# Gated mix of two 32-head attentions on one core: the load order of the first phase, and a scale chain of its own for the values' weights and the gate

## The chip, the cores and the metric

The kernel runs on 1 core of one Trainium2 chip. The metric is the device time of one launch in microseconds (us). The time before is 2800.9 us, the median of 3 runs (2800.7 to 2802.06). A difference of less than 0.2% (5.6 us) counts as no change here.

## The reference, cut to what matters

Two full multi-head attentions A and B read the same x (1 x 2048 x 640); each has its own `wqkv` (640 x 1920) and `wo` (640 x 640), with 32 heads of 20 features. A gate per token, made from x and `gate_w` (640), mixes the two outputs.

```
g = _sigmoid((x * gate_w).sum(-1, keepdims=True))
a = _A_ref(x, A_wqkv, A_wo)
b = _B_ref(x, B_wqkv, B_wo)
return g * a + (1 - g) * b
...
qkv = (...)((x @ wqkv).reshape(B, S, 3, H, Dh), 2, 0, 3, 1, 4)
q, k, v = qkv[0], qkv[1], qkv[2]
scores = jnp.einsum("bhqd,bhkd->bhqk", q, k) * scale
p = _softmax(scores, axis=-1)
o = jnp.einsum("bhqk,bhkd->bhqd", p, v)
```

## The kernel before, in words

**Tiles and stages.** Tokens lie in 16 tiles of 128 (`NT`), features in 5 tiles of 128 (`NC`), queries in 4 blocks of 512 (`QB`). Heads come in groups of 4. After a first phase of about 100 us, the main loop (`for G in range(STEPS + 1)`, L1112) runs 512 steps, in each of which TensorE makes scores (L639), score maxima for later steps (L581), value products (L657) and pieces of projections (L382) in an order written out by hand (`STEP`). ScalarE takes exponentials (L642), VectorE takes maxima (L592, L589).

**Two halves of a float.** Products of weights and x run on float16 pairs: each float32 operand is scaled by a power of two and split into a high part and a low part (`xh`, `xl`; `wbh`, `wbl`; `wvh`, `wvl`). The power of two comes from the largest absolute value. So nothing can be split before its largest value is known on all partitions.

**`scales` (L167)** makes those powers. Its input is a column of per-partition maxima for each tensor (`wm`). TensorE turns them into rows (L173), VectorE takes the maximum of each row (L177), builds powers of two (`powers`, L162 to L165) and a small diagonal matrix `dg` (L183), TensorE multiplies it by ones, which puts the numbers on all partitions (L190), and VectorE copies them out of PSUM (L193). It is a generator: where it says `PRODUCT`, the caller decides when the next TensorE instruction goes into the program.

**The first phase (L833 to L969).** SyncE (queue SP) issues the loads: `ws` (the first group's q and k weights, 2 DMAs of 800 KB), `wv` (the values' weights, 400 KB), `xs` (x, 8 DMAs of 640 KB), then `wstage` (the next group's weights). ScalarE's queue loads the gate's 640 numbers into a column of `wv` (L845), element by element. GpSimd (POOL) fills `mrow` with a constant and copies it by 4 DMAs into rows of the key tiles `KT` (L850). VectorE reduces `ws`, `wv`, the gate column and the 8 pieces of x (`largest`, L234). One call of `scales` then serves five columns: q weights, k weights, values' weights, gate, x.

**The chunks.** `turn` (L863) transposes 4 tiles of x on TensorE (L869); its `drain` scales and splits them on ScalarE (L873) and VectorE (L874). 6 turns are in the program before the scales are known. `a_chunk(ch)` projects 512 tokens on the first group's q and k weights (15 matmuls, L382), and ScalarE and VectorE split the result (L417, L418, tile `cq`). `beside` puts a turn for the next chunk after every second or third matmul. `r_chunk` does the same for the other heads' q features (tile `rk`). The order is: chunk 0, chunk 1, key differences of the first half (POOL, L468 to L472, then DMAs to `kd`), chunk 2, `r_chunk` 0, chunk 3, differences of the second half. Then the values' weights and the gate are split (L945, L946; ScalarE L320, POOL L321, L322), and the first maxima (L581, which read `kd`) start, with the rest of `r_chunk` and the value projections (`project_v`, which read `wvh` and `wvl`) between them. Rows of q and k go to `QT`, `KT` and `KD` by DMAs of SP (L428) and POOL (L430).

**What sets the order.** Each engine runs its instructions in the program's order. PSUM banks are handed out by `take`, which takes the free bank that a planned clock says is free first. The tile `mrow` shares its two buffers with `cq`: the second pair of chunks writes into the buffer that `mrow` had.

Of the kernel before, what the change touches and what calls it, by code (L numbers as in the profile page):

```python
# [14 lines left out]
OP = mybir.AluOpType  # L15
AX = mybir.AxisListType
# [52 lines left out]
def kernel(  # L69
# [163 lines left out]
    def largest(dst, src):  # L233
        nc.vector.tensor_reduce(dst, src, axis=AX.XY, op=OP.max,  # L234
                                apply_absolute_value=True)
        spend("dve", 0.5)
# [602 lines left out]
    w_t = wqkv[0].rearrange("(c p) f -> p c f", p=P)  # L839
    for part in range(2):  # L840
        nc.sync.dma_start(ws[:, part], w_t[:, :, part * D:part * D + 320])
    nc.sync.dma_start(wv[:, :, :160], w_t[:, :, 2 * D:2 * D + 160])
    for i in range(0, NT, 2):
        nc.sync.dma_start(xs[:, i:i + 2, :], x_t[:, i:i + 2, :])
    nc.scalar.dma_start(wv[:, :, 160], gate_w.rearrange("(c p) -> p c", p=P))  # L845
    mrow = wts.tile([P, S], F16, name="mrow", tag="cq", bufs=2)[:4]
    nc.gpsimd.memset(mrow, MS)
    for i in range(2):
        for j in range(2):
            nc.gpsimd.dma_start(KT[i][64 * j + 60:64 * j + 64], mrow.unsqueeze(1).to_broadcast([4, 2, S]))  # L850
    for i in range(2):
        nc.gpsimd.memset(V[i][:, :, :, DH:VW], 1.0)
    xm = start.tile([P, 8], F32, name="xm")
    wm = start.tile([P, 5], F32, name="wm")
    for part in range(2):
        largest(wm[:, part:part + 1], ws[:, part])
    largest(wm[:, 2:3], wv[:, :, :160])
    largest(wm[:, 3:4], wv[:, :, 160:161])
    for i in range(8):
        largest(xm[:, i:i + 1], xs[:, 2 * i:2 * i + 2, :])  # L860
    nc.vector.tensor_reduce(wm[:, 4:5], xm, axis=AX.X, op=OP.max)

    def turn(j0, c):  # L863

# [20 lines left out]
    load()  # L885
    drains = [turn(0, c) for c in range(NC)] + [turn(4, 0)]
    found = []
    run(scales(wm, 5, lambda r, inv: found.extend((r, inv))))
    r, inv = found
    r_x = r[:, 4:5]  # L890
    hi, lo = blk["a", 0] = block_tiles("a")
    split_now(ws[:, 1, :, 0:GF], r[:, 1:2], hi[:, :, 0:GF], lo[:, :, 0:GF])
    split_now(ws[:, 0, :, 0:48], r[:, 0:1], hi[:, :, GF:P], lo[:, :, GF:P])
    for f in drains:
# [5 lines left out]
    nc.gpsimd.tensor_copy(hi.rearrange("p c (j f) -> p c j f", j=4), w_r)  # L900
    nc.gpsimd.tensor_tensor(lo.rearrange("p c (j f) -> p c j f", j=4), w_r, hi.rearrange("p c (j f) -> p c j f", j=4),
                            op=OP.subtract)
    nc.vector.tensor_copy(inv_x, inv[:, 4:5])
    halves = []
    both = cycle((nc.sync, nc.gpsimd))

    def a_chunk(ch):
        if ch % 2 == 0:
            halves.append(half_tiles(0))
        n = slice((ch % 2) * QB, (ch % 2 + 1) * QB)  # L910
        hl = halves[ch // 2][:, :, n]
# [33 lines left out]
    split_now(wv[:, :, :160], r[:, 2:3], hi[:, :, :160], lo[:, :, :160])  # L945
    split_now(wv[:, :, 160:161], r[:, 3:4], hi[:, :, 160:161], lo[:, :, 160:161])  # L946
    nc.vector.tensor_scalar(inv_g, inv[:, 3:4], inv_x, -1.0, op0=OP.mult, op1=OP.mult)
    set_qk(0, r[:, 0:2], inv[:, 0:2])
    set_v(0, r[:, 2:3], inv[:, 2:3])
    split_next()  # L950
    rest = series(*(r_chunk(ch, (0, 1)) for ch in (1, 2, 3)), *(project_v(0, j) for j in range(0, NT, 2)))

# [233 lines left out]
```

## Time and profile before

| what | us |
|---|---|
| median of 3 runs | 2800.9 |
| lowest, highest | 2800.7, 2802.06 |
| the profiled execution's own time | 2800.33 |
| its span, first to last instruction | 2798.5 |
| TensorE busy (PE) | 2744.9 (98%) |
| ScalarE busy (ACT) | 2524.6 (90%) |
| VectorE busy (DVE) | 2452.3 (88%) |
| GpSimd busy (POOL) | 671.9 (24%) |

The profile is of one execution; 1.8 us of its own time lie around the span. Times in rows are us from the span's start. A row of the timeline reads: start, us busy, engine, line, operation, tile written <- tiles read, shapes (partitions x elements), count of merged instructions, and in brackets the idle time before it and what ended it. PE is TensorE's matmuls, PEld its weight loads, SPq, ACTq and POOLq are DMA issues. [...]

### The profile page before, as it was taken

To read this page: it belongs to the slowest core of one execution; us is meant where nothing else is said; L and a number is where in the kernel's file an instruction comes from. 1 tells how busy PE (TensorE), PEld (TensorE's weight loads), DVE (VectorE), ACT (ScalarE), POOL (GpSimd) and SP (SyncE) were. 2 spreads that over 40 slices of the span, in tenths; PEclk is the share of its full clock that TensorE was granted. 3 is DMA by queue.
4 is the path that set the end of the run, shared out by engine and by line. 5 is a ranking of instruction groups with operands and counts; after the bars stand their busy time and mean duration, and the time that the engine had idled before them with its cause. 6 is when DMAs were issued, how large, how long until landed. Compare 5 with 4: busy or idle time off the path is not lost.

```text
span 2798.5 us, 61863 instructions
## 1 busy us (share of the span) xinstructions
PE 2744.9 (98%) x23122; PEld 939.9 (34%) x23122; DVE 2452.3 (88%) x4795; ACT 2524.6 (90%) x5106; POOL 671.9 (24%) x914
## 2 busy tenths in 40 slices
PE   6999999999999999999999999999999999999998
PEld 3433332333333332333333323333333333322222
DVE  6789899889999999888888988989988898999982
ACT  3799999999999999999999889999999999989987
POOL 5322122312222421321221212222342202200111
PEclk9999999999999999999999999999999999999999
DMA  4020102001020211202012231122201112131112
GB/s 136 19 57 14 41 11 46 7 21 25 14 64 17 62 27 54 48 8 61 21 35 70 58 77 31 38 63 54 61 23 42 33 46 63 31 88 55 42 48 75
DMA packets 172943, 124.57 MB, mean 45 GB/s; under 512 B 103264, under 2 KB 142488, under 8 KB 172640
## 3 DMA queue, kind: packets, MB, share of 16 engines
q1 hardware_dynamic: 170096, 118.99, 16.9%
q8 instruction: 181, 2.97, 0.4%
q0 software_dynamic: 1600, 0.96, 0.2%
q14 instruction: 122, 1.00, 0.1%
q10 hardware_dynamic: 944, 0.66, 0.1%
HBM read 54.54 MB, written 31.85 MB: 31 GB/s over the span
## 4 chain that ended last, share of the span: by engine, by line
PE 92%; DVE 3%; ACT 2%; DMA 1%; POOL 1%; issue 1%; SPq 0%; POOLq 0%; ACTq 0%; DVEq 0%
PE acc L657 35%; PE bank L581 19%; PE bank L382 19%; PE bank L639 18%; DVE mpart L592 2%; ACT pt L642 1%; DMA xs<-in_A_x_dram 0%; ACT rl L585 0%; DMA wv<-in_A_wqkv_dram 0%; PE bank L820 0%; DVE rl L589 0%; PE bank L190 0%; SPq L428 0%; DVE ot L743 0%; PE bank L869 0%
## 5 line engine op out<-in xcount | busy, mean ns | idle before, releaser
L642 ACT ACTIVATE pt<-bank 128x512 f32<-128x512 f32 x4096 | 2169.2, 612 | 166.7 <-PE bank L639 101.7
L592 DVE TENSOR_REDUCE mpart<-bank 128x1 f32<-128x512 f32 x2976 | 1865.2, 682 | 222.2 <-PE bank L581 114.8
L657 PE MATMUL acc<-pt,v 128*21 128x512 f32 x8192 | 1082.2, 600 | 0.6 <-DVE ot L743 0.4
L639 PE MATMUL bank<-qt,kt 64*128 64x512 f16 x4096 | 1051.7, 380 | 4.2 <-ACT pt L642 2.0
L581 PE MATMUL bank<-kt,qt 60*128 60x512 f16 x3536 | 1021.3, 380 | 5.1 <-ACT pt L642 1.7
L581 PEld LDWEIGHTS <-qt 60*128 60x128 f16 x4096 | 238.1, 94 | 862.9 <-issue 802.9
L589 DVE CUSTOM_DVE_ANT_0 rl<-bank,rl 128x512 f32<-128x512 f32 x560 | 378.7, 680 | 16.7 <-ACT rl L585 10.6
L585 ACT ACTIVATE rl<-bank 128x512 f32<-128x512 f32 x560 | 329.7, 595 | 10.7 <-PE bank L581 8.7
L639 PEld LDWEIGHTS <-kt 64*128 64x128 f16 x4096 | 235.5, 94 | 238.7 <-issue 122.8
L382 PE MATMUL bank<-xx,wbh 128*128 128x168 f16 (+3 forms) x2400 | 286.0, 239 | 2.6 <-ACT xx L873 1.9
L657 PEld LDWEIGHTS acc<-pt,v 128*21 128x21 f32 x8192 | 143.1, 99 | 428.8 <-issue 421.9
L382 PE MATMUL bank<-xx,wbl 128*128 128x168 f16 (+3 forms) x1200 | 256.1, 237 | 0.0
L751 POOL TENSOR_TENSOR ot<-ot,sq 128x512 f32<-128x512 f32 x63 | 66.0, 1047 | 773.4 <-DVE sq L748 773.4
L382 PEld LDWEIGHTS <-wbh 128*128 128x128 f16 x2400 | 189.4, 98 | 109.5 <-issue 102.0
L581 PE MATMUL bank<-kd,qt 60*128 60x512 f16 x560 | 203.8, 380 | 1.6 <-DMA kd<-dd 1.2
L382 PE MATMUL bank<-woh,o_in 128*128 128x320 f16 (+1 forms) x640 | 156.4, 302 | 5.5 <-DMA o_in<-o_scr 5.4
L411 POOL CAST cq<-fs 128x512 f16<-128x512 f32 x60 | 36.6, 610 | 521.0 <-ACT fs L409 517.4
L382 PE MATMUL bank<-wvh,xx 128*128 128x160 f16 (+1 forms) x1280 | 155.2, 234 | 0.1
L382 PEld LDWEIGHTS <-xx 128*128 128x128 f16 x1920 | 131.5, 97 | 52.3 <-issue 49.1
L382 PE MATMUL bank<-wvl,xx 128*128 128x160 f16 (+1 forms) x640 | 137.3, 231 | 0.5 <-POOL wvl L322 0.5
L382 PEld LDWEIGHTS <-wbl 128*128 128x128 f16 x1200 | 117.4, 98 | 4.3 <-issue 0.8
L382 PEld LDWEIGHTS <-o_in 128*128 128x128 f16 (+1 forms) x960 | 80.9, 97 | 97.7 <-issue 63.8
(131 smaller groups left out, 1259.1 us busy)
## 6 DMA issues: line engine op xcount, KB each, us to landing
y_scr<-y_out SPq DMA_DIRECT2D x48, 320.0 KB
y_out<-y_scr SPq DMA_DIRECT2D x32, 320.0 KB
kt<-cq SPq DMA_DIRECT2D x120, 80.0 KB
o_scr<-on SPq DMA_DIRECT2D x240, 40.0 KB
o_in<-o_scr SPq DMA_DIRECT2D x64, 96.0 KB
kt<-cq SPq DMA_DIRECT2D x136, 40.0 KB
wstage<-in_B_wqkv_dram SPq DMA_DIRECT2D x13, 400.0 KB
xs<-in_A_x_dram SPq DMA_DIRECT2D x8, 640.0 KB
```

Of the source, the lines that this page charges most:

```text
L382: nc.tensor.matmul(out_ap, a, b, start=(k == 0), stop=(k == len(pairs) - 1))
L411: nc.gpsimd.tensor_copy(hi, f)
L581: nc.tensor.matmul(pt, QT[g % 2][r, pair, q0:q0 + P], k, start=True, stop=True)
L585: nc.scalar.activation(relus[u, j], pt, AF.Relu)
L589: nc.vector.tensor_tensor_reduce(rl, pt, rl, 1.0, LOW, OP.add, OP.max, m)
L592: nc.vector.tensor_reduce(m, pt, axis=AX.X, op=OP.max)
L639: nc.tensor.matmul(et, KT[g % 2][r, pair, kt * P:(kt + 1) * P], QT[g % 2][r, pair, qb * QB:(qb + 1) * QB], start=True, stop=True)
L642: nc.scalar.activation(pt, et, AF.Exp, scale=factor(g // 4))
L657: nc.tensor.matmul(acc[32 * h:32 * h + VW, :], V[(g // 2) % 2][:, kt, (g % 2) * GH + h, :], ptiles.pop((G, kk, h)), start=(kt == 0), stop= ...
L751: nc.gpsimd.tensor_tensor(t3, t3, sq.unsqueeze(2).to_broadcast([P, 16, 32]), op=OP.mult)
```

## The change

It has four parts. (1) SP issues the 8 loads of x ahead of the load of `wv`. (2) The gate's load moves on ScalarE's queue from the start to behind the sixth drain. (3) POOL's 4 DMAs of constant rows move from the start to behind the split of the other heads' weights (L901 of before). (4) The maxima of `wv` and of the gate, and their scales, leave the first call of `scales`, which now has 3 columns in place of 5. They get a second call of 2 columns: `largest` twice after chunk 1, then the turn of the maxima (L173), then chunk 2, then the product (L190), then `r_chunk` 0, then the copy (L193). `rv` and `invv` replace columns of `r` and `inv`.

```diff
--- before.py
+++ after.py
@@ -839,26 +839,20 @@
     w_t = wqkv[0].rearrange("(c p) f -> p c f", p=P)
     for part in range(2):
         nc.sync.dma_start(ws[:, part], w_t[:, :, part * D:part * D + 320])
-    nc.sync.dma_start(wv[:, :, :160], w_t[:, :, 2 * D:2 * D + 160])
     for i in range(0, NT, 2):
         nc.sync.dma_start(xs[:, i:i + 2, :], x_t[:, i:i + 2, :])
-    nc.scalar.dma_start(wv[:, :, 160], gate_w.rearrange("(c p) -> p c", p=P))
+    nc.sync.dma_start(wv[:, :, :160], w_t[:, :, 2 * D:2 * D + 160])
     mrow = wts.tile([P, S], F16, name="mrow", tag="cq", bufs=2)[:4]
     nc.gpsimd.memset(mrow, MS)
-    for i in range(2):
-        for j in range(2):
-            nc.gpsimd.dma_start(KT[i][64 * j + 60:64 * j + 64], mrow.unsqueeze(1).to_broadcast([4, 2, S]))
     for i in range(2):
         nc.gpsimd.memset(V[i][:, :, :, DH:VW], 1.0)
     xm = start.tile([P, 8], F32, name="xm")
     wm = start.tile([P, 5], F32, name="wm")
     for part in range(2):
         largest(wm[:, part:part + 1], ws[:, part])
-    largest(wm[:, 2:3], wv[:, :, :160])
-    largest(wm[:, 3:4], wv[:, :, 160:161])
     for i in range(8):
         largest(xm[:, i:i + 1], xs[:, 2 * i:2 * i + 2, :])
-    nc.vector.tensor_reduce(wm[:, 4:5], xm, axis=AX.X, op=OP.max)
+    nc.vector.tensor_reduce(wm[:, 2:3], xm, axis=AX.X, op=OP.max)
 
     def turn(j0, c):
 
@@ -885,9 +879,9 @@
     load()
     drains = [turn(0, c) for c in range(NC)] + [turn(4, 0)]
     found = []
-    run(scales(wm, 5, lambda r, inv: found.extend((r, inv))))
+    run(scales(wm, 3, lambda r, inv: found.extend((r, inv))))
     r, inv = found
-    r_x = r[:, 4:5]
+    r_x = r[:, 2:3]
     hi, lo = blk["a", 0] = block_tiles("a")
     split_now(ws[:, 1, :, 0:GF], r[:, 1:2], hi[:, :, 0:GF], lo[:, :, 0:GF])
     split_now(ws[:, 0, :, 0:48], r[:, 0:1], hi[:, :, GF:P], lo[:, :, GF:P])
@@ -900,7 +894,11 @@
     nc.gpsimd.tensor_copy(hi.rearrange("p c (j f) -> p c j f", j=4), w_r)
     nc.gpsimd.tensor_tensor(lo.rearrange("p c (j f) -> p c j f", j=4), w_r, hi.rearrange("p c (j f) -> p c j f", j=4),
                             op=OP.subtract)
-    nc.vector.tensor_copy(inv_x, inv[:, 4:5])
+    nc.vector.tensor_copy(inv_x, inv[:, 2:3])
+    nc.scalar.dma_start(wv[:, :, 160], gate_w.rearrange("(c p) -> p c", p=P))
+    for i in range(2):
+        for j in range(2):
+            nc.gpsimd.dma_start(KT[i][64 * j + 60:64 * j + 64], mrow.unsqueeze(1).to_broadcast([4, 2, S]))
     halves = []
     both = cycle((nc.sync, nc.gpsimd))
 
@@ -937,16 +935,28 @@
     beside(a_chunk(0), 2, turns_of(4, range(1, NC)))
     beside(a_chunk(1), 3, turns_of(8))
     differences_of(0, KD[0])
+    largest(wm[:, 3:4], wv[:, :, :160])
+    largest(wm[:, 4:5], wv[:, :, 160:161])
+    of_v = []
+    chain = scales(wm[:, 3:5], 2, lambda r, inv: of_v.extend((r, inv)))
+    while next(chain) is not PRODUCT:
+        pass
+    next(chain)
     beside(a_chunk(2), 3, turns_of(12))
+    while next(chain) is not PRODUCT:
+        pass
+    next(chain)
     run(r_chunk(0, (1,)))
+    run(chain)
+    rv, invv = of_v
     run(a_chunk(3))
     differences_of(1, KD[1])
     hi, lo = v_tiles(0)
-    split_now(wv[:, :, :160], r[:, 2:3], hi[:, :, :160], lo[:, :, :160])
-    split_now(wv[:, :, 160:161], r[:, 3:4], hi[:, :, 160:161], lo[:, :, 160:161])
-    nc.vector.tensor_scalar(inv_g, inv[:, 3:4], inv_x, -1.0, op0=OP.mult, op1=OP.mult)
+    split_now(wv[:, :, :160], rv[:, 0:1], hi[:, :, :160], lo[:, :, :160])
+    split_now(wv[:, :, 160:161], rv[:, 1:2], hi[:, :, 160:161], lo[:, :, 160:161])
+    nc.vector.tensor_scalar(inv_g, invv[:, 1:2], inv_x, -1.0, op0=OP.mult, op1=OP.mult)
     set_qk(0, r[:, 0:2], inv[:, 0:2])
-    set_v(0, r[:, 2:3], inv[:, 2:3])
+    set_v(0, rv[:, 0:1], invv[:, 0:1])
     split_next()
     rest = series(*(r_chunk(ch, (0, 1)) for ch in (1, 2, 3)), *(project_v(0, j) for j in range(0, NT, 2)))
```

The order of all other instructions on every engine is the same as before. The banks differ in the first phase and are the same up to renaming behind it. Two places follow.

TensorE from the end of chunk 1 to the start of chunk 2, before (`bank_93` holds chunk 1, `bank_95` chunk 2, L869 is a turn of x):

```order
L382 LDWEIGHTS wbl
L382 MATMUL bank_93<-xx,wbl 128x512
L869 MATMUL bank_92<-ident,xs 128x128 x4
L382 LDWEIGHTS wbh [waits DVE_49]
L382 MATMUL bank_95<-xx,wbh 128x512 [waits Activation_49]
```

The same place of the change (L863 is the turn of x, `bank_94` holds chunk 2):

```order
L382 LDWEIGHTS wbl
L382 MATMUL bank_93<-xx,wbl 128x512
L863 MATMUL bank_92<-ident,xs 128x128 x4
L173 MATMUL bank_95<-ident,wm 2x128 [waits DVE_49]
L382 LDWEIGHTS wbh
L382 MATMUL bank_94<-xx,wbh 128x512 [waits Activation_49]
```

The turn of the two maxima stands between the chunks and waits for VectorE.

TensorE from the end of chunk 2 to the start of `r_chunk` 0, before (`bank_95` chunk 2, `bank_93` `r_chunk` 0):

```order
L382 MATMUL bank_95<-xx,wbl 128x512
L869 MATMUL bank_92<-ident,xs 128x128 x4
L382 LDWEIGHTS wbh [waits Pool_49]
L382 MATMUL bank_93<-xx,wbh 128x512 [waits DVE_49]
L382 LDWEIGHTS wbh
```

The same place of the change (`bank_94` chunk 2, `bank_90` `r_chunk` 0):

```order
L382 MATMUL bank_94<-xx,wbl 128x512
L863 MATMUL bank_93<-ident,xs 128x128 x4
L190 MATMUL bank_89<-dg,ones 128x2 [waits DVE_49] x2
L382 LDWEIGHTS wbh [waits Pool_49]
L382 MATMUL bank_90<-xx,wbh 128x512
```

The product that spreads the scales stands between them and waits for VectorE's `dg`.

VectorE of the change behind chunk 1 (L418 splits the chunk's result, L868 the next turn of x):

```order
L868 SCALAR_TENSOR_TENSOR xx<-bank_92,both,xx 128x512 [waits Activation_49]
L418 SCALAR_TENSOR_TENSOR cq<-bank_93,cq 128x512 [waits Activation_49]
L234 TENSOR_REDUCE wm<-wv 128x1 [waits DMAHW2_49]
L234 TENSOR_REDUCE wm<-wv 128x1 [waits DMAHW5_49]
L868 SCALAR_TENSOR_TENSOR xx<-bank_89,both,xx 128x512 [waits Activation_49]
```

The two reductions on which L173 waits stand behind the L418 of chunk 1.

VectorE of the change behind chunk 2, up to the L418 of `r_chunk` 0:

```order
L418 SCALAR_TENSOR_TENSOR cq<-bank_94,cq 128x512 [waits DMASW2_49,DMASW1_49,DMASW3_49,DMASW0_49,Activation_49]
L177 TENSOR_REDUCE e<-bank_95 2x1
L162 TENSOR_SCALAR e<-e 2x1 [waits DVE_49]
L163 TENSOR_SCALAR e<-e 2x1 [waits DVE_49]
L164 TENSOR_SCALAR e<-e 2x1 [waits DVE_49]
L165 TENSOR_SCALAR e<-e 2x1
L183 TENSOR_SCALAR dg<-ident,e 2x2 [waits DVE_49] x2
L418 SCALAR_TENSOR_TENSOR rk<-bank_90,rk 128x512 [waits Activation_49]
```

Before, these two L418 are followed by the next turn's L874 and by the next L418; the steps from `e` to `dg`, on which L190 waits, stand behind the L418 of chunk 2.

## The prediction

> **What bounds the kernel now.** I read the page's busy line and chain of waits, then the timeline of the first 75 us, since all edits lie there.
>
> ```profile
> PE 2744.9 (98%) x23122; PEld 939.9 (34%) x23122; DVE 2452.3 (88%) x4795; ACT 2524.6 (90%) x5106; POOL 671.9 (24%) x914
> PE 92%; DVE 3%; ACT 2%; DMA 1%; POOL 1%; issue 1%; SPq 0%; POOLq 0%; ACTq 0%; DVEq 0%
> ```
>
> TensorE carries 92% of the chain, and the order behind the first phase is unchanged. So whatever the first phase gains or loses when the first maxima start arrives at the end one for one. In the first phase the chain runs through DMA, as the chain in order of time shows:
>
> ```profile
> 1.79 11.17 DMA wv<-in_A_wqkv_dram
> 12.97 12.94 DMA xs<-in_A_x_dram
> 25.93 1.50 DVE xm L234
> 29.27 1.03 PE bank L190 x4
> ```
>
> **The loads: a gain of 5.0 us.** VectorE's timeline shows when each load had landed:
>
> ```profile
> 6.25 1.82 DVE L234 TENSOR_REDUCE wm<-ws 128x1 f32<-128x1600 f32 x1 [4.69 <-DMA ws<-in_A_wqkv_dram]
> 9.50 1.82 DVE L234 TENSOR_REDUCE wm<-ws 128x1 f32<-128x1600 f32 x1 [1.43 <-DMA ws<-in_A_wqkv_dram]
> 12.98 1.05 DVE L234 TENSOR_REDUCE wm<-wv 128x1 f32<-128x800 f32 x2 [1.65 <-DMA wv<-in_A_wqkv_dram]
> 14.73 10.98 DVE L234 TENSOR_REDUCE xm<-xs 128x1 f32<-128x1280 f32 x7 [0.70 <-DMA xs<-in_A_x_dram]
> 25.93 1.49 DVE L234 TENSOR_REDUCE xm<-xs 128x1 f32<-128x1280 f32 x1 [0.23 <-DMA xs<-in_A_x_dram]
> ```
>
> The first seven pieces of x take 1.58 us apiece (10.98 / 7, with 1.49 of work in each), the pace of the DMA: 640 KB in 1.58 us are 415 GB/s. The last piece lands at 25.93 and sets the scales. The rates by stretch (last column GB/s, before it the DMA share):
>
> ```profile
> 2.00:4.00 2.00, 0.00 (x0) 0.00 (x0) 0.00 (x0) 0.00 (x0) 1.69 (x2) 1.00 0.85 229
> 4.00:6.00 2.00, 0.00 (x0) 0.00 (x0) 0.00 (x0) 0.00 (x0) 2.00 (x5) 1.00 0.83 229
> 6.00:8.00 2.00, 0.00 (x0) 0.00 (x0) 1.75 (x1) 0.00 (x0) 0.69 (x3) 1.00 1.05 380
> 8.00:10.00 2.00, 0.00 (x0) 0.00 (x0) 0.57 (x2) 0.45 (x1) 0.00 (x0) 1.00 1.19 212
> 10.00:12.00 2.00, 0.00 (x0) 0.00 (x0) 1.32 (x1) 0.83 (x1) 0.00 (x0) 1.00 1.08 219
> 14.00:16.00 2.00, 0.66 (x2) 0.29 (x2) 1.30 (x2) 0.00 (x0) 0.00 (x0) 1.00 1.02 415
> ```
>
> From 8 to 12 the engines are busy but move half as much: there the values' weights and POOL's constant rows are under way. The queues' shares in the first 24 us, POOL's (q0) and the gate's (q10):
>
> ```profile
> q0 software_dynamic: 192, 0.13, 3.5%
> q10 hardware_dynamic: 656, 0.00, 1.5%
> ```
>
> Lower end: only the moved bytes go. The values' 0.41 MB at 415 GB/s are 1.0 us; 3.5% and 1.5% of 24 us are 0.84 and 0.36: together 2.2 us. Upper end, from zero: 0.46 MB have moved by 4.0; the other 1.18 MB of q and k weights at 380 GB/s end at 7.1, and 5.24 MB of x at 415 GB/s take 12.6, so the last byte moves at 19.7. The first weights (0.82 MB, moved by about 5.6 at these rates) landed at 6.25, 0.7 later; so x lands at 20.4, a gain of 5.5. VectorE keeps up: its second weight reduction would end near 9.6, where the first x lands. I take **5.0**, near the upper end, since the slow stretch ends when those packets end and the rate is even behind it.
>
> **First new wait: 3.5 us.** In the times of before, the end of chunk 1:
>
> ```profile
> 43.96 0.60 PE L869 MATMUL bank<-ident,xs 128*128 128x128 f32 x4
> 44.40 0.81 PE L382 MATMUL bank<-xx,wbh 128*128 128x512 f16 x3
> 45.32 0.75 DVE L874 SCALAR_TENSOR_TENSOR xx<-bank,both,xx 128x512 f16<-128x512 f32 x1 [0.33 <-ACT xx L873]
> 45.99 0.68 DVE L418 SCALAR_TENSOR_TENSOR cq<-bank,cq 128x512 f16<-128x512 f32 x1
> ```
>
> Chunk 2 began at 44.40. Now L173 stands ahead of it and waits for the two reductions of `wv`, which stand behind the L418 of chunk 1 on VectorE. L418 ends at 46.67, and the next VectorE work can start 0.07 before that (as 45.99 lies before the end of 45.32's 0.75): 46.60. The 1.05 for both reductions give 47.65, and L173 starts about 0.05 later, 47.7. L173 holds TensorE for 0.2 us:
>
> ```profile
> 128.06 0.27 PE L173 MATMUL bank<-ident,m 128*1 128x128 f32 x1
> 128.26 1.06 PE L657 MATMUL acc<-pt,v 128*21 128x512 f32 x8
> ```
>
> 47.9 less 44.4 is **3.5**. Behind the waiting instruction are chunk 2's 15 matmuls and 5 turns; ScalarE's and VectorE's drains wait for those.
>
> **Second new wait: 3.9 us.** The end of chunk 2, the chain of the first scales, and a warm L190 later in the run:
>
> ```profile
> 49.82 2.32 PE L382 MATMUL bank<-xx,wbh 128*128 128x512 f16 x10
> 51.41 0.68 DVE L418 SCALAR_TENSOR_TENSOR cq<-bank,cq 128x512 f16<-128x512 f32 x1
> ...
> 28.08 0.28 DVE L177 TENSOR_REDUCE e<-bank 5x1 f32<-5x128 f32 x1 [0.47 <-PE bank L173]
> 29.27 1.01 PE L190 MATMUL bank<-dg,ones 5*128 5x5 f32 x4 [1.23 <-DVE dg L183]
> ...
> 134.91 0.60 PE L190 MATMUL bank<-dg,ones 1*128 1x1 f32 x4
> 135.44 1.06 PE L657 MATMUL acc<-pt,v 128*21 128x512 f32 x8
> ```
>
> `r_chunk` 0 began at 49.82. Now L190 stands ahead and needs `dg`, whose steps stand behind chunk 2's L418. L177 can start at 52.02 (51.41 + 0.68 - 0.07); 1.19 later (28.08 to 29.27) L190 starts, 53.21; it holds TensorE 0.53 (134.91 to 135.44): 53.74, so **3.9**. Behind it are `r_chunk` 0 and chunk 3, 30 matmuls. The last step, L193, is waited for only by the split of `wv`, 6 us later.
>
> **What covers a part: 1.2 us.**
>
> ```profile
> 57.62 0.50 PE L581 MATMUL bank<-kd,qt 60*128 60x512 f16 x2 [1.16 <-DMA kd<-dd]
> 73.28 0.23 PE L382 MATMUL bank<-wvl,xx 128*128 128x161 f16 x1 [0.55 <-POOL wvl L322]
> ```
>
> Before, TensorE waited 1.16 us for `kd`. That chain (chunk 1, POOL's differences, DMAs) isn't behind the new waits, so this wait goes: what is late next is TensorE itself, 7.4 late on it. The second wait stays: POOL's row of work from chunk 3 to `wvl` shifts with chunk 3. So 7.4 - 1.2 = 6.2 arrive.
>
> **Costs of nothing.** POOL's four DMA issues (2.51 us in the row below) fall before chunk 0's rows at 40.06, where 0.77 were idle, and delay them by 1.7; POOL then idled 2.77 before 46.06, which hides it, and `kd` now has 6 us to spare. The gate's issue (0.48 us, one element each) stands before a drain that waited 0.35 for TensorE; 0.13 are left, which I leave to the range. Uncovered, these would be 1.7 and 0.5. `wv` and the gate are needed 20 us after they now land. I take scales of 3 and 2 columns to be as long as those of 5: L177 above reduces its 5 rows side by side. What they may save is inside 0.1 us.
>
> ```profile
> 3.46 2.51 POOL L850 DMA_DIRECT2D kt<-mrow  x4 [0.31 <-POOL mrow L847]
> 40.06 0.62 POOL L430 DMA_DIRECT2D kt<-cq  x1 [0.77 <-ACT cq L417]
> 46.06 1.00 POOL L430 DMA_DIRECT2D kt<-cq  x2 [2.77 <-ACT cq L417]
> 35.93 0.69 ACT L873 ACTIVATE xx<-bank,both 128x512 f16<-128x512 f32 x1 [0.35 <-PE bank L869]
> ```
>
> **The clock: 3.1 us.** Stretches of 3.41 us (the third column from the end is the granted clock):
>
> ```profile
> 56.04:59.46 3.42, 2.26 (x12) 0.72 (x10) 2.19 (x12) 2.62 (x5) 3.42 (x7) 1.00 0.38 90
> 96.99:100.41 3.42, 2.59 (x12) 0.74 (x9) 2.04 (x5) 3.15 (x8) 0.00 (x0) 1.00 0.48 120
> 100.41:103.82 3.41, 3.40 (x17) 1.86 (x17) 2.96 (x6) 2.94 (x6) 0.00 (x0) 0.50 0.00 0
> ```
>
> Behind the stretch to 100.41, in which TensorE was busy 2.59 of 3.42 with products of 60 and 64 rows, the clock was halved for 3.41 us. Behind the stretch from 56.04, busy less (2.26) but mostly with 128 rows, it stayed. Weighted by rows, the first did about 31% of a full stretch's work, the second 52%; the bound lies between. The new gaps are 3.3 us (44.40 to 47.7) and 3.4 (49.82 to 53.21, with only tiny products in the next 0.5). A gap of 3.3 cut evenly by a stretch's border leaves 51% in each half, any other cut less in one. So I expect a halved clock behind each gap. Each costs 1.7 us (half of 3.41) at most, 1.55 where the gap's tail lies in the halved stretch: 3.1 for two, between 0 and 3.4.
>
> [...]
>
> **The sum**: -5.0 + 3.5 + 3.9 - 1.2 + 3.1 = +4.3 us. The profiled execution's own 2800.33 becomes 2804.6; the median shown, 2800.9, is 0.6 above it, so I predict **2805.2** for the median.
>
> **The rivals.**
> - *The clock doesn't fall*: +1.2, so 2802.1. [...] Against it: the row to 100.41. Chance 0.18.
> - *Slower, since x doesn't come earlier by as much as said*: if the slow stretch from 8 to 12 belongs to the change from small rows to x's long ones, only 2.2 us are gained and the sum is +7.1, 2808.0. It decides from a gain under 3.7 us: 9.3 less 3.7 is 5.6 us, 0.2%. For it: the engines were busy there. Against it: the stretch ends with POOL's packets. Chance 0.16.
> - *TensorE doesn't wait at L173 and L190*, because something hides it: -5.0 + 0.7 (their own time), less nothing for `kd`, whose chain moves too: 2796.6. Against it: each stands directly between two chunks on an engine that runs in order. Chance 0.04.
>
> **How the numbers follow.** My forecast has 0.62: both waits, at least one fall of the clock, a gain of 4 to 5.5; it spans 2803 to 2806.8. About a fifth of it, and nearly all of the second rival, lie above 2806.5, where slower by over 0.2% begins (about what a measurement of this kernel can tell from no change): 0.13 + 0.14 = 0.27. Faster by over 0.2% (under 2795.3) needs the third rival and more, 0.04. Within 0.2%: 0.69. The range takes in the rivals of the clock and most of the load's: 2800.5 to 2808.0.
>
> **What would show it.** The last x reduction starts near 21 in place of 25.93; L234 of `wv` stands directly ahead of L173, with some 3 us of TensorE's idle before it; the same before L190, released by `dg` (L183); no wait for `kd`; a granted clock of 0.50 in a stretch of 3.4 us behind each gap. First maxima at about 58.8 + 3.1 in place of 57.62 (which is the sum once more). I would be wrong if x lands later than 22, if a wait at L417 for the constant rows' buffer appears, or if the later part of the run doesn't carry the shift to the end.

## The result, and the profile after

The changed kernel takes **2806.06 us** (median of 22 runs, 2803.54 to 2808.72) against 2801.97 us for the kernel before in the same rounds (22 runs, 2799.98 to 2804.85). The ratio is **1.0016**, with a 95% interval of 1.001 to 1.0022: 4.1 us slower, against a forecast of 4.3. That is under the 0.2% which this document counts as a change, though the interval lies clear of 1.

The profiled execution lies in the upper part of the 22: its own time is 2807.79 us, 1.7 over the median, while the profiled execution of before (2800.33) lies 1.6 under the median of before. So its span of 2806.0 is 7.5 over the span of before, where the medians differ by 4.1. Rows of this profile below are those of a slower execution than the typical one, and the clock has a part in that: the mean granted clock is 0.993 in it and 0.995 in that of before. The page's busy line and its chain of waits:

```profile
PE 2752.7 (98%) x23127; PEld 943.2 (34%) x23127; DVE 2452.0 (87%) x4803; ACT 2524.2 (90%) x5106; POOL 671.7 (24%) x914
PE 91%; DVE 3%; ACT 2%; DMA 1%; SPq 1%; issue 1%; POOL 0%; POOLq 0%; ACTq 0%; DVEq 0%
```

TensorE still sets the end. Its busy time rose by 7.8 us with five instructions more, which is a first hint at its clock: the same matmuls took longer (the first ten of `r_chunk` 0 take 4.45 us in a row below, 2.32 before).

**The loads.** VectorE's timeline of the changed kernel:

```profile
7.89 1.82 DVE L234 TENSOR_REDUCE wm<-ws 128x1 f32<-128x1600 f32 x1 [0.42 <-DMA ws<-in_A_wqkv_dram]
9.63 10.82 DVE L234 TENSOR_REDUCE xm<-xs 128x1 f32<-128x1280 f32 x7
20.61 1.49 DVE L234 TENSOR_REDUCE xm<-xs 128x1 f32<-128x1280 f32 x1 [0.16 <-DMA xs<-in_A_x_dram]
...
42.57 1.04 DVE L234 TENSOR_REDUCE wm<-wv 128x1 f32<-128x800 f32 x2
```

The last piece of x lands at 20.61 in place of 25.93, 5.3 us earlier (5.0 expected). The first seven follow the weights without a wait. The table by stretch (before the last column the share of the DMA engines, in the last GB/s) shows that the stretch of half rate from 8 to 12 us is gone:

```profile
6.00:8.00 2.00, 0.00 (x0) 0.00 (x0) 1.58 (x2) 0.06 (x1) 0.00 (x0) 1.00 1.07 387
8.00:10.00 2.00, 0.41 (x2) 0.29 (x2) 2.00 (x2) 1.23 (x1) 0.00 (x0) 1.00 1.04 422
10.00:12.00 2.00, 1.16 (x6) 0.91 (x5) 2.00 (x2) 0.00 (x0) 0.00 (x0) 1.00 1.02 412
```

422 and 412 GB/s stand where 212 and 219 stood, though the engines are no busier (1.04 and 1.02, for 1.19 and 1.08).

**The two waits.** TensorE's timeline:

```profile
39.95 0.60 PE L863 MATMUL bank<-ident,xs 128*128 128x128 f32 x4
43.67 0.37 PE L173 MATMUL bank<-ident,wm 128*2 128x128 f32 x1 [3.12 <-DVE wm L234]
43.83 1.49 PE L382 MATMUL bank<-xx,wbh 128*128 128x512 f16 x3
...
50.16 0.60 PE L863 MATMUL bank<-ident,xs 128*128 128x128 f32 x4
53.89 1.01 PE L190 MATMUL bank<-dg,ones 2*128 2x2 f32 x4 [3.13 <-DVE dg L183]
54.83 4.45 PE L382 MATMUL bank<-xx,wbh 128*128 128x512 f16 x10
...
64.05 0.39 PE L581 MATMUL bank<-kd,qt 60*128 60x512 f16 x2
```

Each of the two products idles TensorE for 3.1 us, and the brackets name VectorE's steps as the releasers. The reductions of `wv` start at 42.57, behind the L418 of chunk 1, though the last byte of the loads had moved by 22.5 us and the gate's numbers by 27.3: the wait is for VectorE's place in its queue, not for data. The first maxima start at 64.05 with no wait for `kd`, 6.4 later than before (57.62).

**The clock.** Windows of 1 us (third column from the end: the granted clock):

```profile
43.00:44.00 1.00, 0.33 (x2) 0.26 (x3) 0.61 (x2) 0.00 (x0) 1.00 (x3) 0.57 0.24 52
45.00:46.00 1.00, 1.00 (x6) 0.82 (x5) 0.00 (x0) 0.00 (x0) 0.92 (x2) 0.50 0.29 72
46.00:47.00 1.00, 1.00 (x5) 0.50 (x4) 0.07 (x1) 0.69 (x1) 0.92 (x2) 0.72 0.18 43
...
53.00:54.00 1.00, 0.11 (x1) 0.11 (x1) 0.86 (x7) 0.00 (x0) 1.00 (x3) 0.69 0.37 87
58.00:59.00 1.00, 1.00 (x4) 0.30 (x2) 0.00 (x0) 0.00 (x0) 0.00 (x0) 0.50 0.00 0
60.00:61.00 1.00, 1.00 (x6) 0.44 (x5) 0.00 (x0) 0.08 (x1) 0.00 (x0) 0.90 0.00 0
```

From the values between 0.50 and 1.00 the ends of the slow stretches can be worked out: 0.57 means that 0.86 of 43 to 44 ran at half clock, so it fell near 43.1; 0.72 puts its return near 46.6. That is one stretch of 3.4 us. Behind the second gap it fell near 53.4 and came back near 60.2: two stretches, 6.8 us. All falls and returns of this trace lie whole multiples of 3.41 apart: falls at 19.25, 43.14, 53.38 and 107.99 in the first 112 us, returns at 32.90, 46.55, 60.21 and 111.41, with a mean clock of 1.00 or 0.50 from each to the next. So do those of before, on borders of their own (falls at 25.31 and 100.41, returns at 35.55 and 103.82). With the matmuls at about half their pace in these stretches (4.45 us for 2.32), the two falls could cost up to half of 10.2 us in this execution, 5.1, where 3.1 was expected.

### The profile page after: what moved, and what is told of

Same layout as the page of the kernel before. It is cut to its first block, busy times and chain, and to the rows that moved or that the text cites. A ratio compares the mean times of both kernels' runs of the same rounds, so it can differ in the third digit from the quotient of the medians.

```text
span 2806.0 us, 61882 instructions
## 1 busy us (share of the span) xinstructions
PE 2752.7 (98%) x23127; PEld 943.2 (34%) x23127; DVE 2452.0 (87%) x4803; ACT 2524.2 (90%) x5106; POOL 671.7 (24%) x914
## 4 chain that ended last, share of the span: by engine, by line
PE 91%; DVE 3%; ACT 2%; DMA 1%; SPq 1%; issue 1%; POOL 0%; POOLq 0%; ACTq 0%; DVEq 0%
PE acc L657 34%; PE bank L382 19%; PE bank L581 19%; PE bank L639 18%; DVE mpart L592 2%; ACT pt L642 1%; DMA xs<-in_A_x_dram 0%; ACT rl L585 0%; PE bank L820 0%; SPq L430 0%; DVE rl L589 0%; SPq L428 0%; PE bank L190 0%; DMA ws<-in_A_wqkv_dram 0%; PE bank L863 0%
## 5 line engine op out<-in xcount | busy, mean ns | idle before, releaser
L657 PE MATMUL acc<-pt,v 128*21 128x512 f32 x8192 | 1082.7, 600 | 0.6 <-DVE ot L743 0.4
L581 PE MATMUL bank<-kt,qt 60*128 60x512 f16 x3536 | 1021.6, 381 | 5.2 <-ACT pt L642 1.7
L581 PEld LDWEIGHTS <-qt 60*128 60x128 f16 x4096 | 238.2, 94 | 862.8 <-issue 802.5
L382 PE MATMUL bank<-xx,wbh 128*128 128x168 f16 (+3 forms) x2400 | 290.2, 241 | 2.6 <-ACT xx L867 1.9
L657 PEld LDWEIGHTS acc<-pt,v 128*21 128x21 f32 x8192 | 143.1, 99 | 428.6 <-issue 422.0
L382 PE MATMUL bank<-xx,wbl 128*128 128x168 f16 (+3 forms) x1200 | 256.9, 238 | 0.0
L382 PEld LDWEIGHTS <-wbh 128*128 128x128 f16 x2400 | 190.3, 98 | 111.3 <-issue 104.7
L581 PE MATMUL bank<-kd,qt 60*128 60x512 f16 x560 | 203.4, 379 | 0.5
L382 PE MATMUL bank<-woh,o_in 128*128 128x320 f16 (+1 forms) x640 | 156.4, 302 | 5.4 <-DMA o_in<-o_scr 5.4
L382 PE MATMUL bank<-wvh,xx 128*128 128x160 f16 (+1 forms) x1280 | 155.2, 234 | 0.1
L382 PEld LDWEIGHTS <-xx 128*128 128x128 f16 x1920 | 131.5, 97 | 51.6 <-issue 48.5
L382 PE MATMUL bank<-wvl,xx 128*128 128x160 f16 (+1 forms) x640 | 137.3, 231 | 0.0
L382 PEld LDWEIGHTS <-wbl 128*128 128x128 f16 x1200 | 117.7, 98 | 5.0 <-issue 2.2
L382 PEld LDWEIGHTS <-o_in 128*128 128x128 f16 (+1 forms) x960 | 80.9, 97 | 97.6 <-issue 64.2
```

Source lines behind the costliest of these rows:

```text
L382: nc.tensor.matmul(out_ap, a, b, start=(k == 0), stop=(k == len(pairs) - 1))
L581: nc.tensor.matmul(pt, QT[g % 2][r, pair, q0:q0 + P], k, start=True, stop=True)
L657: nc.tensor.matmul(acc[32 * h:32 * h + VW, :], V[(g // 2) % 2][:, kt, (g % 2) * GH + h, :], ptiles.pop((G, kk, h)), start=(kt == 0), stop= ...
```

## The experiments

The theory is that of the prediction: x gains by the transfers that were ahead of it, the two products on TensorE cost their waits in full, and the clock falls behind each. Its rivals were that the clock costs nothing, that the gain of x has another source, and that a third cause (the moved loads themselves, for one) makes the time. Each run is compared with the kernel before on the same chip (medians of 2801.58, 2801.8 and 2801.06 us in the three sessions). The change itself was measured once, beside a median of 2801.97, so a difference between a run and the change can be off by up to 0.9 us.

**1. Both waits taken away** (`late_products`). The transposed maxima (L173) go behind chunk 2, the spreading product (L190) behind `r_chunk` 0, so that VectorE's steps have a chunk of matmuls to hide behind:

```diff
-    next(chain)
     beside(a_chunk(2), 3, turns_of(12))
+    next(chain)
     while next(chain) is not PRODUCT:
         pass
-    next(chain)
     run(r_chunk(0, (1,)))
+    next(chain)
     run(chain)
```

> The change with L173 moved behind chunk 2 and L190 behind r_chunk 0, so that TensorE meets both when their inputs are done. Theory (the loads give 5.3 us, the two waits take 3.5 and 3.9 us and bring two falls of the clock): both waits and both falls go, the products' own 0.7 us stay, and the wait for kd is back with about 0.5 us. First maxima at 57.6 - 5.3 = 52.3 (up to 1.5 later by the clock's phase in chunk 0), time 5 us under before, about 2797 (2796 to 2798.5). Rival A (earlier loads don't arrive at the end): within 1 us of before, 2802. Rival B (the 4 us come from elsewhere than the two waits): still 2805 to 2806.

Measured: **2797.2 us** (2795.39 to 2798.95), ratio 0.9984, interval 0.9975 to 0.9993. That is 8.9 us less than the change, and faster than both kernels. TensorE's timeline of it:

```profile
45.66 0.27 PE L173 MATMUL bank<-ident,wm 128*2 128x128 f32 x1
49.77 0.60 PE L190 MATMUL bank<-dg,ones 2*128 2x2 f32 x4 [0.61 <-DVE dg L183]
53.73 0.51 PE L581 MATMUL bank<-kd,qt 60*128 60x512 f16 x2
```

The first maxima start 10.3 us earlier than in the change and 3.9 earlier than before. So all of the loss sits in the place of the two products. The wait for `kd` that was expected back (about 0.5 us) isn't there; L190 waits 0.61 us for `dg` in its place.

**2. One wait taken away at a time** (`late_turn` moves only L173, `late_spread` only L190; each is one half of the diff above).

> The change with only L173 moved, behind chunk 2; L190 stays directly behind it and waits. Theory: the first wait (3.5 us, with 1.4 of the clock behind it in the profiled run) goes, the second stays 3.9 us with its fall of the clock: 2806.1 - 4.5 = 2801.5 (2800 to 2803). Rival (the two waits hide one another, so that one alone costs as much as both): 2805 to 2806.

> The change with only L190 moved, behind r_chunk 0 (its inputs are made where they were); L173 stays between chunks 1 and 2 and waits. Theory: the second wait (3.9 us) and the clock behind it (2.7 in the profiled run) go, the first (3.5, with 1.4 of the clock) stays: 2806.1 - 5.5 = 2800.5 (2799 to 2802). With late_turn's 4.5 the two single moves should add up to about the 8.9 us of late_products. Rival (the waits hide one another): 2805 to 2806.

Measured: `late_turn` 2801.61 us (ratio 1.0003, 0.9994 to 1.0012), `late_spread` 2801.14 us (0.9999, 0.999 to 1.0008). Against the change they gain 4.5 and 4.9; together 9.4, near the 8.9 of both. The waits add up to within 0.5 us, so neither hides much of the other. (With L173 late, L190's wait is 3.94 us long in the trace, not 3.13.) The granted clock of `late_turn`, and then that of `late_spread`, by windows:

```profile
50.00:51.00 1.00, 1.00 (x5) 0.72 (x5) 0.00 (x0) 0.00 (x0) 1.00 (x3) 0.50 0.09 21
55.00:56.00 1.00, 1.00 (x4) 0.30 (x3) 0.00 (x0) 0.00 (x0) 0.00 (x0) 0.50 0.21 49
```

```profile
45.00:46.00 1.00, 1.00 (x5) 0.79 (x4) 0.00 (x0) 0.00 (x0) 0.92 (x2) 0.50 0.27 69
52.00:56.00 4.00, 4.00 (x21) 2.00 (x20) 2.75 (x11) 0.70 (x2) 2.71 (x6) 1.00 0.34 80
```

Between 38 and 64 us the clock falls behind the gap that is left, and only there: for two stretches in `late_turn` (49.2 to 56.1) and for one in `late_spread` (43.3 to 46.7).

**3. The clock alone** (`filled_gaps`). The waits stay, but TensorE is kept busy in them by 14 matmuls of 512 columns ahead of each of the two products. Nobody reads their results:

```diff
+    def warm(n):
+        i, pt = take()
+        for _ in range(n):
+            tick_block(T_SCORE, free_at[i])
+            nc.tensor.matmul(pt, blk["a", 0][0][:, 0, :], xh[:, 0, 0:QB], start=True, stop=True)
+        give(i, clock["done"])
...
+    warm(14)
     next(chain)
```

> The change with 14 matmuls of 128 rows and 512 columns, whose results nobody reads, ahead of L173 and 14 ahead of L190: 14 x 0.215 = 3.0 us of work in each gap, inside the 3.1 us of waiting. The waits themselves stay as long. Theory: the granted clock stays at 1.00 behind both gaps, and the time falls by the price of the clock, 3 us (2 to 4.5), to about 2803, with a smaller spread of the runs than the change's 2803.5 to 2808.7. Rival (the clock costs nothing, the waits are all): 2806, as the change, or above it by what the added work delays. If the added work delayed L190 or L173, their start would show it.

Measured: **2802.67 us** (2801.03 to 2803.2), ratio 1.0002, 0.9993 to 1.0011. The timeline, and the clock by windows of 4 us:

```profile
39.82 3.19 PE L939 MATMUL bank<-xx,wbh 128*128 128x512 f16 x14
48.63 3.18 PE L939 MATMUL bank<-xx,wbh 128*128 128x512 f16 x14
59.04 0.39 PE L581 MATMUL bank<-kd,qt 60*128 60x512 f16 x2
```

```profile
42.00:46.00 4.00, 3.90 (x23) 2.23 (x22) 1.80 (x4) 1.11 (x2) 3.18 (x6) 1.00 0.31 75
54.00:58.00 4.00, 4.00 (x20) 1.84 (x19) 0.76 (x2) 0.60 (x1) 1.16 (x3) 1.00 0.27 64
```

The fill takes the place of the idle time (3.2 us each, against waits of 3.1), so TensorE comes to its own work no sooner; yet the time falls by 3.4 us (by 3.0 when each of the two is taken against the kernel before of its own session). So the clock costs 3.0 to 3.4 us in the median. The spread is smaller too: 2.2 us in 11 runs, against 5.2 in 22. That fits a clock that falls differently from run to run, since the runs' mean granted clock is 0.992 to 0.996 in the change and 0.995 in ten of these eleven; but the kernel before, which has no such gaps, spreads by 4.9 us in its 22 runs, so the clock behind the gaps is not shown to be the only cause. Against `late_products`, in the same session, the waits themselves cost 5.5 us.

**4. How little work is too little** (`filled_32_rows`: the same 28 matmuls on 32 of 128 rows; `filled_half`: 7 full ones in each gap in place of 14).

```diff
-            nc.tensor.matmul(pt, blk["a", 0][0][:, 0, :], xh[:, 0, 0:QB], start=True, stop=True)
+            nc.tensor.matmul(pt, blk["a", 0][0][:32, 0, :], xh[:32, 0, 0:QB], start=True, stop=True)
```

```diff
-    warm(14)
+    warm(7)
```

> As filled_gaps (14 products of 512 columns that nobody reads ahead of each of the two products with transposed maxima), but each of the 28 uses only 32 of TensorE's 128 rows. TensorE is as busy as in filled_gaps, with a quarter of the array's rows at work. Theory, that the grant follows the work weighted by rows: the clock falls to 0.50 behind the gaps as in the change; the time is about 2806 us (2805 to 2807). Rival, that it follows mere busy time: the clock stays at 1.00 from 38 to 64 us, and the time is that of filled_gaps, 2802.7 us.

> As filled_gaps, but 7 of the unread products instead of 14 in each gap: 1.6 us of each 3.1-us gap are filled, 1.5 us stay idle, so that any stretch of 3.4 us holds at least about 53% of full work. Theory, that the clock falls only where a stretch holds less than the trace of before bounds (between 31% and 52% of full work): the clock stays at 1.00 behind both gaps, and the time is that of filled_gaps, about 2802.7 us (2801.5 to 2804). Rival, that half a stretch idle is enough: the clock falls to 0.50 behind a gap in some runs, and the time is 2803 to 2806 us with a wider spread.

Measured: `filled_32_rows` 2805.08 us (2801.76 to 2807.05), ratio 1.0014, 1.0005 to 1.0023. Its windows:

```profile
51.00:52.00 1.00, 1.00 (x6) 0.43 (x5) 0.95 (x4) 0.00 (x0) 1.00 (x3) 1.00 0.35 76
52.00:53.00 1.00, 1.00 (x7) 0.46 (x5) 0.66 (x5) 0.00 (x0) 1.00 (x3) 1.00 0.44 100
53.00:54.00 1.00, 1.00 (x6) 0.51 (x6) 0.00 (x0) 0.00 (x0) 1.00 (x3) 0.80 0.42 106
54.00:55.00 1.00, 1.00 (x4) 0.40 (x3) 0.00 (x0) 0.00 (x0) 0.21 (x1) 0.50 0.35 82
57.00:58.00 1.00, 1.00 (x6) 0.49 (x5) 0.00 (x0) 0.00 (x0) 0.00 (x0) 0.99 0.23 48
```

TensorE was busy in the whole of each of these windows and lost its clock all the same, for one stretch, behind the second gap. So in this run busy time alone did not keep the clock up. Behind the first gap the clock stayed at 1.00 in this execution. By windows of 4 us and the ones above, the clock of this run fell near 19.4, 53.6 and 104.8 and came back near 33.1 and 57.0, again whole multiples of 3.41 apart. Borders counted back from 53.60 in steps of 3.41 tell the two gaps apart, if work is weighted by rows, which is the author's estimate. From 39.95 to 43.36 TensorE worked 0.68 us with 128 rows and 2.73 us with 32, which is 40% of a full stretch's work when it is weighted by rows. From 50.19 to 53.60 it worked 2.45 us with 32 rows, 0.53 us in L190 with 2 rows and 0.43 us with 128, which is 31%.

Worked out the same way, the unfilled gaps behind which the clock fell left a stretch with 0 to 24% of full work. (In `old_loads`, `rows_gate_early` and `values_first` the clock and the borders are an estimate from the matmuls' lengths: the first three of L382 behind the first gap take 0.81, 0.81 and 1.49 us, where they take 0.81 in `filled_gaps` at 1.00 and 1.49 in the change at 0.50.) But the first gap, 3.12 us long in each, kept its clock in `old_loads` (44%) and in `rows_gate_early` (45%), where a border cuts it, and lost it in the change (24%), in `values_first` (20%) and in `late_spread` (20%). So by this estimate the same gap cost its clock or not by where the borders lay. The weight is not exact: among products of 60 and 64 rows, the same working gives about 37% ahead of the fall at 100.41 of before (TensorE busy 2.59 of 3.41 us), where the prediction had 31%, and about 42% ahead of the fall at 107.99 of the change (2.96 of 3.41).

`filled_half` took 2804.66 us (2802.5 to 2805.59), ratio 1.001, 1.0001 to 1.0019, and fell into two groups: four runs at 2802.5 to 2802.96 with a mean granted clock of 0.995, seven at 2804.5 to 2805.59 with 0.993 or 0.994. The profiled run is of the first group, and its clock stayed at 1.00 behind both gaps; windows of the second gap:

```profile
50.00:51.00 1.00, 0.10 (x1) 0.00 (x0) 0.97 (x4) 0.00 (x0) 1.00 (x4) 1.00 0.00 0
51.00:52.00 1.00, 0.29 (x3) 0.29 (x3) 0.72 (x6) 0.00 (x0) 1.00 (x3) 1.00 0.41 88
```

The time of 2804.66 us lies outside the theory's range (2801.5 to 2804) and inside the rival's, and the expectation that the clock stays up failed in most runs, as far as time and mean clock tell. The expectation's 53% left something out: L190 follows on the second gap for 0.53 us with products of 2 rows, so 1.61 + 0.53 = 2.14 of 3.41 us can be nearly without work, and 37% of full work is left. That lies inside the prediction's bounds (31% to 52%), so they stand. Which of the gaps the clock falls behind in the seven runs is not shown, since none of them has a trace.

**5. Which of the moved transfers held x back.** `old_loads` takes the whole order of loads back and keeps the second chain. `rows_gate_early` takes only POOL's rows and the gate back to the start, `values_first` only the order of `wv` and x. `before_rows_late` is the kernel before with only POOL's four DMAs moved. In `values_first` and `old_loads` the load of `wv` goes back ahead of x:

```diff
+    nc.sync.dma_start(wv[:, :, :160], w_t[:, :, 2 * D:2 * D + 160])
     for i in range(0, NT, 2):
         nc.sync.dma_start(xs[:, i:i + 2, :], x_t[:, i:i + 2, :])
-    nc.sync.dma_start(wv[:, :, :160], w_t[:, :, 2 * D:2 * D + 160])
```

In `rows_gate_early` and `old_loads` the gate and the rows go back to the start (and are taken away behind the split); `before_rows_late` does the reverse with the kernel before, for the three lines of the rows alone:

```diff
+    nc.scalar.dma_start(wv[:, :, 160], gate_w.rearrange("(c p) -> p c", p=P))
     mrow = wts.tile([P, S], F16, name="mrow", tag="cq", bufs=2)[:4]
     nc.gpsimd.memset(mrow, MS)
+    for i in range(2):
+        for j in range(2):
+            nc.gpsimd.dma_start(KT[i][64 * j + 60:64 * j + 64], mrow.unsqueeze(1).to_broadcast([4, 2, S]))
```

> The change with the loads, the gate and the constant rows in the order and places of before: only the second chain of scales is left of the change. Theory: the last piece of x is reduced at 25.9 again, less nothing, since the two weight reductions of wv ahead of x waited for the DMA anyway; the time is the change's plus 5.3 us, about 2811.3 (2810 to 2813), the waits ahead of L173 and L190 3.1 us each. Rival A (earlier loads don't arrive at the end): 2806, as the change.

> The change with the gate's load and POOL's constant rows back at the start; x stays ahead of wv. Theory 1 (the constant rows slow the 16 DMA engines from 8 to 12 us, and the values' 0.41 MB are worth only their 1.0 us): the last piece of x is reduced near 24.7, the time is about 2810 (4 us above the change). Theory 2 (the slow stretch belongs to the values' short rows): the last piece near 21.8 (0.84 + 0.36 us later than the change's 20.6), the time 2807.3.

> The change with wv ahead of x again; the gate and the constant rows stay late. Theory 1 (constant rows make the slow stretch): the last piece of x is reduced 1.0 to 1.3 us later than the change's 20.6, near 21.8, the time about 2807.3. Theory 2 (the values' short rows make it): near 24.5, the time about 2810.

> The kernel before with one edit: POOL's four DMAs of constant rows stand where the change has them; one chain of scales for five columns, wv and the gate ahead of x as before. No new wait. Theory 1: the slow stretch from 8 to 12 goes, the last piece of x is reduced near 22.9 in place of 25.9, and the time falls by about 3 us to 2798.6 (2797.5 to 2800). Theory 2 (the slow stretch belongs to the values' rows): 0.8 us earlier, 2801.

The start of the last x reduction in each profile, and the medians:

| kernel | last x reduction starts | us | ratio to before, 95% interval |
|---|---|---|---|
| before | 25.93 | | 1 |
| old_loads | 25.67 | 2813.39 | 1.0043, 1.0029 to 1.0057 |
| rows_gate_early | 24.6 | 2809.65 | 1.0032, 1.0021 to 1.0042 |
| before_rows_late | 22.55 | 2799.63 | 0.9993, 0.9984 to 1.0002 |
| values_first | 21.94 | 2808.97 | 1.0023, 1.0014 to 1.0032 |
| the change | 20.61 | 2806.06 | 1.0016, 1.001 to 1.0022 |

VectorE's rows for x in `rows_gate_early` (first piece, then the other seven, of which the last starts 1.49 before 26.06), and its rates:

```profile
12.65 1.49 DVE L234 TENSOR_REDUCE xm<-xs 128x1 f32<-128x1280 f32 x1 [1.64 <-DMA xs<-in_A_x_dram]
15.04 11.02 DVE L234 TENSOR_REDUCE xm<-xs 128x1 f32<-128x1280 f32 x7 [0.91 <-DMA xs<-in_A_x_dram]
```

```profile
8.00:10.00 2.00, 0.00 (x0) 0.00 (x0) 0.81 (x1) 0.77 (x1) 0.00 (x0) 1.00 1.10 328
10.00:12.00 2.00, 0.00 (x0) 0.00 (x0) 1.01 (x1) 0.52 (x1) 0.00 (x0) 1.00 1.03 204
```

With POOL's rows and the gate back, the stretch of half rate is back (204 GB/s), and now it is x that it slows. Without them but with `wv` ahead of x, the rate from 8 to 12 is 406 and 412:

```profile
8.00:10.00 2.00, 0.00 (x0) 0.00 (x0) 1.78 (x1) 1.28 (x1) 0.00 (x0) 1.00 1.10 406
10.00:12.00 2.00, 0.66 (x2) 0.28 (x2) 1.21 (x1) 0.00 (x0) 0.00 (x0) 1.00 1.01 412
```

So the slow stretch belongs to those small transfers and not to the passage from small rows to x's long ones. Of the 5.3 us, POOL's rows hold 3.4 (25.93 to 22.55), the gate about 0.6 (22.55 to 21.94), `wv` 1.3 (21.94 to 20.61). The gate's part is a difference of two runs with different programs behind it, and it was not tried alone. `before_rows_late`, which has the gate's load and `wv` at the start and only the rows late, runs at 379 and 412 GB/s from 8 to 12, so most of the slow stretch belongs to the rows.

x landed where it was expected in these runs, but not every time did. `values_first` is 1.7 us over the 2807.3 that was expected, and 2.9 over the change for an x that is 1.3 later; `old_loads`, with five runs only, lies above its range of 2810 to 2813. What made this excess isn't shown. The clock may have a part in it: four of the five runs of `old_loads` are slower than the traced one, three of them with a lower mean clock (0.992, for 0.994).

`before_rows_late` also showed what the move of the rows costs where nothing hides it. Its timelines of VectorE, TensorE and POOL, and its list of DMA issues (count, KB each, median us from issue to landing):

```profile
22.55 1.49 DVE L234 TENSOR_REDUCE xm<-xs 128x1 f32<-128x1280 f32 x1 [0.20 <-DMA xs<-in_A_x_dram]
56.04 0.50 PE L581 MATMUL bank<-kd,qt 60*128 60x512 f16 x2 [2.69 <-DMA kd<-dd]
42.85 0.51 POOL L430 DMA_DIRECT2D kt<-cq  x1 [1.57 <-DMA kt<-mrow]
```

```profile
kt<-mrow POOLq DMA_DIRECT2D x4, 32.0 KB, 6.1
```

x gained 3.4 us, the first maxima only 1.6 (57.62 to 56.04): POOL's next row DMAs wait for the rows of constants to land, the key differences follow later, and the wait for `kd` grows from 1.16 to 2.69 us. Behind that wait the matmuls are slower as well: six of L382 take 2.74 us from 56.69, where six take 1.47 from 59.58 in `filled_gaps` at a clock of 1.00, and four take 1.04 again from 60.21. By the author's estimate that is one stretch at 0.50. In the change the same wait on POOL is there, and is covered:

```profile
40.94 0.51 POOL L430 DMA_DIRECT2D kt<-cq  x1 [1.55 <-DMA kt<-mrow]
```

## Why the prediction was right, point by point

- **The bound.** Right: what the first maxima lose arrives at the end. In the profile they start 6.43 later, and the first scales of the main loop (L173, 128.06 before) start at 134.54, 6.48 later. By the end of the span it is 7.5. Of the last 1.0, 0.5 arises between 1618 and 1691 us (the value products, L657, go from 6.46 to 6.95 later there); in that time the clock is at 0.50 for 6.8 us in both profiles, from 1653.5 before and from 1661.1 in the change. Another 0.1 comes by 2483, and the rest behind the last value products. The first phase isn't shown to cause this part.
- **The loads, 5.0.** x landed 5.3 earlier, and by the cause that the prediction chose. Its lower end of 2.2 had priced POOL's rows by their packets' share of the queues, 0.84 us. They cost 3.4, four times that: here the share of a queue's own packets did not hold what they did to the other loads.
- **The first wait, 3.5.** Chunk 1's last turn is 4.01 earlier than before (39.95 for 43.96) and chunk 2 only 0.57 (43.83 for 44.40): 3.4.
- **The second wait, 3.9.** Two rows of before, the last turn of chunk 2 and the end of chunk 3:

```profile
49.38 0.60 PE L869 MATMUL bank<-ident,xs 128*128 128x128 f32 x4
55.22 1.24 PE L382 MATMUL bank<-xx,wbl 128*128 128x512 f16 x5
```

Chunk 2's last turn is 0.78 later than before (50.16 for 49.38), `r_chunk` 0 5.01 later (54.83 for 49.82): 4.2. Of the excess, 0.4 is L190 itself, which held TensorE for 0.94 (53.89 to 54.83) and not 0.53, since the clock had fallen before it.
- **The cover, 1.2.** The wait for `kd` went, as said. The second wait, 0.55 for `wvl`, went too, where the prediction had it stay; no row of the changed kernel's value products shows a wait. That brought no time at the end: ahead of it the weights of the second maxima (L581, 65.99) waited 0.4 us for rows of `qt` that a DMA brings, and at 105 us the value products (L657) are 6.47 later, no less than the first maxima.
- **The clock, 3.1.** In the median 3.0 to 3.4, by `filled_gaps`. In the one profile it was more, and there the step that priced each fall as one stretch failed: the second fall lasted two. In its first stretch, 53.38 to 56.79, `r_chunk` 0 ran only from 54.83, 57% of the stretch, and the clock came back behind the next stretch, which was full; chunk 2 had filled 85% of the stretch from 43.14, and one was enough there. Behind the second gap the fall lasted two stretches in four of the five traces that have it unfilled (the change, `values_first`, `old_loads`, `late_turn`: the first ten matmuls of `r_chunk` 0 take 4.45 us in each) and one in `rows_gate_early` (3.69 us, for 2.33 in `filled_gaps` at 1.00). The step that expected a fall behind each gap holds for the second gap in all five, and for the first in three of five (experiment 4). By the rows, chunk 2 took 1.35 longer than before (from 0.57 earlier to 0.78 later) and `r_chunk` 0 with chunk 3 2.6 longer: they began 5.01 later and ended 7.65 later (64.05, for 56.40 before: there chunk 3's last row ends at 56.46, and records overlap by about 0.06, as 59.10 and 59.04 do in `filled_gaps`). With the 0.4 in L190 that is 4.4. The profile also lost clock where the prediction had not looked. The clock is at 0.50 when chunk 0 starts in both kernels. A window of the changed kernel, and then one of the kernel before, show where it came back:

```profile
32.00:33.00 1.00, 1.00 (x5) 0.58 (x4) 0.27 (x1) 0.50 (x1) 0.92 (x2) 0.55 0.00 0
```

```profile
35.00:36.00 1.00, 1.00 (x7) 0.83 (x6) 1.00 (x2) 0.65 (x2) 1.00 (x2) 0.72 0.00 0
```

That is 32.9 us in place of 35.6, 2.7 earlier, while chunk 0 started 5.3 earlier (26.83 for 32.16). So chunks 0 and 1 gave back 1.3 of the 5.3 ahead of the first gap. With it the clock cost 5.7 us in this profile, and the first maxima start at 64.05 where the prediction said about 61.9.

- **The sum.** Without the clock +1.2 was expected; `filled_gaps` is 1.1 over its session's before. With it +4.3; the median is 4.1 over. That they agree to 0.2 is in part luck. That the waits and the falls of the clock cost time is shown, but chunk 0's clock was not in the sum and a fall was priced too short; in the profiled execution these make the first maxima 2.1 us later than said, and how they balance in the median isn't shown.
- **The weight by rows.** The clock fell behind 3.1 us of idle time, of which no more than 2.6 lay in one stretch of the change, and in `filled_32_rows` behind none. As far as these runs show, a stretch with too little work, weighted by rows, was enough (31% in `filled_32_rows`, 0 to 24% in the unfilled gaps); the weight by rows is the author's estimate from few traces and was not swept.
- **Costs of nothing.** The four issues on POOL cost nothing here, but the landing behind them was not priced: 5.8 us from issue to landing in the change (6.1 in `before_rows_late`), for which later DMAs of POOL wait (1.55 us ahead of 40.94). The spare 6 us of `kd` hid it, and that spare time is the loss at the two products. Scales of fewer columns are no shorter at L177: 0.27 to 0.28 us with 2, 3 and 5 rows.

## What to carry to other kernels

A small product between two chunks on the busiest engine cost the chain ahead of it here, 3.1 us of idle TensorE each time, so give that chain a chunk of work to hide behind: moving two calls by one chunk each turned 4.1 us of loss into 4.4 us of gain (each under 0.2% of the run). Price a gap on TensorE with the clock it may lose behind it, as a range of none, one or two stretches of 3.4 us, which are what these traces show, and compare medians, since one profile is one execution (7.5 us between the two spans here, 4.1 between the medians). Where DMA engines are busy but move half as many bytes, as from 8 to 12 us of before (shares of 1.19 and 1.08 at 212 and 219 GB/s), look for small transfers beside the large ones and try moving those first; here that was worth 3.4 us to the last piece of x.

## What the runs showed of the hardware

- Four DMAs of 32 KB into 4 partitions each, with the gate's single elements, held the loads beside them to 204 to 219 GB/s for some 2 to 4 us (8 to 12 us of before, 10 to 12 of `rows_gate_early`), where the same loads ran at 406 to 422 GB/s without them (8 to 12 us of the change and of `values_first`), while the share of busy engines was no lower (1.03 to 1.19, for 1.01 to 1.10). With the gate's load and without the four, the rates were 379 and 412 (`before_rows_late`).
- The same four DMAs landed 5.8 us (the change) and 6.1 us (`before_rows_late`) after their issue, where the DMA moved 33 and 27 GB/s in the mean from 24 to 46 us, and 7.1 us beside the loads of before.
- In the traces of before and of the change the granted clock took only 1.00 and 0.50, and inside the spans its stretches at 0.50 were 3.41, 6.83, 10.24 and 13.65 us long. At 0.50 ten matmuls of 512 columns took 4.45 us, at 1.00 2.32.
- Work being weighted by rows (an estimate), the clock fell in the gaps where a stretch held up to 31% of full work, and stayed where each held 40% or more. A stretch at 0.50 with 56 to 60% of full work behind a gap was followed by another (the change, `values_first`, `old_loads`, `late_turn`), one with 82% or more was not (`rows_gate_early`, `late_spread`, and chunk 2 of the change).
- Full occupation with matmuls of 32 rows did not keep the clock up behind the second gap (0.50 from 53.60 to 57.02, `filled_32_rows`); with matmuls of 128 rows in half of each gap it stayed at 1.00 in the traced run of `filled_half`, and by time and mean clock (2802.5 to 2802.96 us, 0.995) in three more of the eleven.
